# The first norm's scale and shift as columns, applied where the transposed tiles leave PSUM

## The chip, the cores and the metric

One core of a Trainium2 chip runs the whole kernel. The metric is the device time of one execution in microseconds (us). TensorE (PE) multiplies, VectorE (DVE), ScalarE (ACT) and GpSimd (POOL) do the work on rows of numbers, and SyncE (SP) issues the transfers (DMA).

## The reference

A transformer block in float32: a layer norm whose scale and shift come from a condition `c`, attention over the last 512 cached keys, a second norm of the same kind, and a gated feed-forward layer. Only the first norm matters here:

```
mod = (silu(c) @ w_mod).reshape(1, 6, 1, 576)       # c: 1 x 576, w_mod: 576 x 3456
sa, ca, ga, sb, cb, gb = mod[:, 0], ..., mod[:, 5]
h = layernorm(x) * (1 + ca) + sa                    # x: 2048 x 576
x = x + ga * attention(h)                           # 32 heads of 128, q = h @ wq
```

## The kernel before

**Blocks and layout.** The 2048 rows of `x` are four blocks of 512 (b = 0 to 3), each of four tiles of 128 rows (t = 0 to 3). The 576 channels are four chunks of 128 and a tail of 64 (k = 0 to 4); the tail is kept twice, on both halves of the 128 partitions. The projection to q needs the normed block with channels on partitions, `hTs[b]`, split in two parts whose sum is the float32 value: `hi` (rounded to the fast matmul format, fp32r) and `lo` (the rest). `pairs_a` multiplies them with a split of `wq`, chunk by chunk in the order lo, hi with k ascending, so `qproj` can begin as soon as chunk 0 is there.

**The steps.** Attention is a loop over steps n, four steps to a pair of a head and a block (a unit); there are 128 units and N = 512 steps. In step n PE does a quarter of the q projection of the unit after next (`qproj`), the scores of step n + 2 (`scores`), the transposes of the probabilities of step n (`transp`) and a quarter of the product with the values of the unit before (`pv`). DVE takes the row maximum (`neg`), the rest of the split (`ptt`, and `qt` after each fourth quarter of `qproj`), ACT the exponentials (`pp`) and the rounded parts. `at_n` and `at_late` put other work at the head or at the end of a step. `ps_qp` is one PSUM bank, so the next unit's projection waits until DVE has read the one before. `st` has four banks, `ot` two, `wo` one.

**Order.** Until step 8 each engine runs its instructions in the order of the program text (`Ordered`). From then on the scheduler may move instructions, except that those given to `keep_order` or `pin` stay behind the instruction written in front of them on their engine.

**The first norm, blocks 0 and 1.** `silu(c)` is made as five columns `cexp` and spread by ACT to 128 equal columns, `sbc`. `mod_mm` multiplies `sbc` (stationary) with rows of `w_mod` (`WM`, moving, 288 columns at a time), once for the scale (m = 1) and once for the shift (m = 0), 10 products each; a float32 product counts as two instructions. The result is the row of 576 numbers on all partitions. `ln_scaled` norms a tile on ACT and multiplies it by the scale row on DVE or POOL. `ln_channels` transposes chunk by chunk. The shift row is turned into five columns `scol` by small transposes, and `ln_shifted` adds the column while the chunk leaves PSUM: ACT writes `hi`, DVE writes `lo` out of PSUM. Block 1 is done in steps 2 to 6 (`ln_scaled` at the end of steps 2 and 3, `chunks1` in steps 5 and 6).

**Blocks 2 and 3.** `norm_block` puts the statistics, `ln_apply` (DVE subtracts and multiplies, POOL multiplies by the scale row and adds the shift row), `ln_ends` (ACT copies the tail) and `ln_transpose` (a tile at a time; four chunks in one PSUM bank, the tail in `wo`) into the 34 steps ahead of n1 = N / 2 = 256. The second half of the units, which reads these blocks, has its projections from step n1 - 7 on.

**Background.** From step 9 on jobs split later weights (`bg_sums` and `bg_split` on POOL and ACT), with the tiles `xs[b]` of finished blocks as room.

Of the kernel before, what the change touches and what calls it, by code (L numbers as in the profile page):

```python
# [44 lines left out]
def adaln_block_kernel(ctx: ExitStack, tc: tile.TileContext, x, k_cache, v_cache, wq, wo, w_gate, w_up, w_down,  # L45
                       c, w_mod, out):
    early = [True]
    nc = Ordered(tc, early, tc.nc)
# [20 lines left out]
    const = ctx.enter_context(tc.tile_pool(name="const", bufs=1))  # L69
# [30 lines left out]
    def f32(ap):  # L100
        return ap.bitcast(F32)
# [66 lines left out]
    xs = []  # L168
# [5 lines left out]
        t = slice(0, TPB) if t is None else t  # L174
        keep_order(nc.sync.dma_start(xs[b][:, t], xf[b][:, t]))

    LN, HH = {}, {}

    def ln_stats(b, t, hold=False):
        if t == 0 and b % 2 == 0:  # L180
# [38 lines left out]
    def ln_apply(b, t, scale_, shift_, mul, add):  # L219
        mv, y = LN[b][:2]  # L220
        h = h_tile("h")
        nc.vector.tensor_scalar(h, xs[b][:, t, :], mv[:, t, 0:1], y[:, t : t + 1], op0=OP.subtract, op1=OP.mult)
        mul.tensor_mul(h, h, scale_)
        add.tensor_add(h, h, shift_)
        HH[b, t] = h

    ENDS = {}

    def ln_ends(b, t):
        ENDS[b, t] = wp.tile([P, 2, TAIL], F32, tag="hd", name="hd", bufs=2)  # L230
        keep_order(nc.scalar.activation(ENDS[b, t], HH[b, t][:, None, NC * P :].to_broadcast([P, 2, TAIL]), AF.Copy))

    def ln_transpose(b, t):
        main, tail = hTs[b]
        h, ends = HH.pop((b, t)), ENDS.pop((b, t))
        cols = slice(t * P, (t + 1) * P)
        p, pt = ps_pt(), ps_wo()
        for k in range(NC):
            nc.tensor.transpose(p[:, k * P : (k + 1) * P], h[:, k * P : (k + 1) * P], ident)
        nc.tensor.transpose(pt[:, :P], ends.rearrange("p s d -> p (s d)"), ident)  # L240
        src = p.rearrange("p (k q) -> p k q", k=NC)
        keep_order(nc.scalar.activation(main[:, :NC, cols], src, AF.Copy))
        nc.vector.tensor_sub(main[:, NC:, cols], src, f32(main[:, :NC, cols]))
        keep_order(nc.scalar.activation(tail[:, 0, cols], pt[:, :P], AF.Copy))
        nc.vector.tensor_sub(tail[:, 1, cols], pt[:, :P], f32(tail[:, 0, cols]))
# [63 lines left out]

    sbc = at.tile([P, NC + 1, P], F32, tag="qt", name="sbc", bufs=2)
    extra = at.tile([P, 4 * P], F32, tag="rb", name="extra", bufs=2)
    scale, shift = mod_rows("scale"), mod_rows("shift")
    WM, EARLY, HN, NMR = {}, {}, {}, {}

    def load_mod(m, ks):
# [3 lines left out]
            kk = P if k < NC else TAIL  # L321
            nc.sync.dma_start(WM[m][:kk, k, :], w_mod[k * P : k * P + kk, m * D : (m + 1) * D])

    def mod_mm(m, ks, p2):
        for k in ks:
            kk = P if k < NC else TAIL
            for j in range(2):
                nc.tensor.matmul(p2[j], sbc[:kk, k, :], WM[m][:kk, k, j * D2 : (j + 1) * D2],
                                 start=(k == 0), stop=(k == NC))

    def ln_scaled(b, t, eng):
        h = h_tile("h")
        nc.scalar.activation(h, xs[b][:, t, :], AF.Identity, scale=LN[b][1][:, t : t + 1],
                             bias=NMR[b][:, t : t + 1])
        eng.tensor_mul(h, h, scale)
        HN[b, t] = h

    def ln_tail(b, t):
        e = extra[:, t * P : (t + 1) * P].rearrange("p (s d) -> p s d", s=2)
        nc.gpsimd.tensor_copy(e, HN[b, t][:, None, NC * P :].to_broadcast([P, 2, TAIL]))  # L340

    def ln_channels(b, t, k, p):
        src = HN[b, t][:, k * P : (k + 1) * P] if k < NC else extra[:, t * P : (t + 1) * P]
# [32 lines left out]
    for j in range(2):  # L376
        nc.scalar.activation(scale[:, j * D2 : (j + 1) * D2], p2[j], AF.Copy, bias=1.0)
# [7 lines left out]
    p2 = [ps_wo(), ps_qp()[:, :D2]]  # L385
# [6 lines left out]
    nc.scalar.activation(shift[:, :D2], p2[0], AF.Copy)  # L392
    nc.vector.tensor_copy(shift[:, D2:], p2[1])
    ends = wp.tile([P, 2, TAIL], F32, tag="hd", name="hd", bufs=2)
    nc.scalar.activation(ends, p2[1][:, None, D2 - TAIL :].to_broadcast([P, 2, TAIL]), AF.Copy)
    pc = ps_qp()
    for k in range(NC + 1):
        src = shift[0:1, k * P : (k + 1) * P] if k < NC else ends.rearrange("p s d -> p (s d)")[0:1, :]
        nc.tensor.transpose(pc[:, k : k + 1], src, ident[0:1, 0:1])
    scol = csb  # L400
    nc.vector.tensor_copy(scol, pc[:, : NC + 1])
# [208 lines left out]
    def at_n(n, fn, *args):  # L610
        at_step.setdefault(n, []).append((fn, args))
# [3 lines left out]
    def at_late(n, fn, *args):  # L615
        at_end.setdefault(n, []).append((fn, args))
# [39 lines left out]
    for i in range(3):  # L656
        at_late(i, ln_some, 1, False, (0, 6, 9)[i], (6, 9, 13)[i])
    for t in range(TPB):
        at_late(2 + t // 2, ln_scaled, 1, t, nc.vector if t % 2 else nc.gpsimd)
    for t in range(TPB):  # L660
        at_n(4, ln_tail, 1, t)
    at_n(5, chunks1, (0, 1))
# [20 lines left out]
        for t in range(TPB):  # L683
            at_n(N // 2 - 59 + 8 * b + t, load_x, b, t)

    def norm_block(b, n_stats, n_apply, n_t, step, sc_, sh_, mul, add):
        for t in range(TPB):
            at_n(n_stats + t, ln_stats, b, t)
            at_n(n_apply + t * step, ln_apply, b, t, sc_, sh_, mul, add)
            at_n(n_t + t * step - 1, ln_ends, b, t)  # L690
            at_n(n_t + t * step, ln_transpose, b, t)
        if b % 2:
            for k in range(6):
                at_n(n_stats + TPB + k, ln_some, b, True, 2 * k, 2 * k + 2, True)
        at_n(n_t - 1, new_hT, b)

    n1 = N // 2
# [81 lines left out]
    def bg_view(b, off, shape):  # L779
        n = 1  # L780
        for d in shape:
            n *= d
        v = xs[b].rearrange("p t d -> p (t d)")[:, off : off + n]
        if len(shape) == 1:
            return v
        names = "abc"[: len(shape)]
        return v.rearrange(f"p ({' '.join(names)}) -> p {' '.join(names)}",
                           **{names[i]: shape[i] for i in range(len(shape) - 1)})
# [738 lines left out]
```

## Time and profile before

| | us |
|---|---|
| time, median of 3 runs (3051.73 to 3054.39) | 3053.7 |
| the profiled execution, its time | 3053.7 |
| its span, from the first to the last instruction | 3051.9 |
| PE busy | 3014.0 |
| DVE busy | 2110.7 |
| ACT busy | 1691.8 |
| POOL busy | 1654.8 |

Times inside the execution count from the start of the span. The granted clock is the share of full speed that TensorE was given: 1.00 is 2.4 GHz, 0.50 is 1.2 GHz, values between are means over a stretch that holds both. PEld is TensorE's loading of the stationary operand, which overlaps the products. "Idle before" is the idle time of an engine just ahead of an instruction, with what ended it.

### The profile page before, as it was taken

To read this page: it belongs to the slowest core of one execution; us is meant where nothing else is said; L and a number is where in the kernel's file an instruction comes from. 1 tells how busy PE (TensorE), PEld (TensorE's weight loads), DVE (VectorE), ACT (ScalarE), POOL (GpSimd) and SP (SyncE) were. 2 spreads that over 40 slices of the span, in tenths; PEclk is the share of its full clock that TensorE was granted. 3 is DMA by queue.
4 is the path that set the end of the run, shared out by engine and by line. 5 is a ranking of instruction groups with operands and counts; after the bars stand their busy time and mean duration, and the time that the engine had idled before them with its cause. 6 is when DMAs were issued, how large, how long until landed. Compare 5 with 4: busy or idle time off the path is not lost.

```text
span 3051.9 us, 49183 instructions
## 1 busy us (share of the span) xinstructions
PE 3014.0 (99%) x16639; PEld 2591.7 (85%) x16639; DVE 2110.7 (69%) x3716; ACT 1691.8 (55%) x3430; POOL 1654.8 (54%) x1544
## 2 busy tenths in 40 slices
PE   8999999999999999999999999999999999999998
PEld 6888888887888788888999988888888888888887
DVE  5666666677666666667888867666666866666667
ACT  5666667656666666555444654444444545444442
POOL 2343457735577787411555127666655666555654
PEclk9999999999999999999999999999999999999999
DMA  3677777776687777775447656555655565555453
GB/s 111 187 197 199 207 228 216 242 207 180 190 244 228 238 243 250 215 216 180 182 161 306 236 177 187 160 150 159 185 145 143 164 189 140 146 145 143 138 156 98
DMA packets 485788, 571.32 MB, mean 187 GB/s; under 512 B 52000, under 2 KB 434208, under 8 KB 476832
## 3 DMA queue, kind: packets, MB, share of 16 engines
q1 hardware_dynamic: 484400, 567.65, 61.8%
q8 instruction: 132, 2.16, 0.3%
q14 instruction: 120, 0.98, 0.1%
q10 hardware_dynamic: 1136, 0.53, 0.1%
HBM read 394.33 MB, written 173.70 MB: 186 GB/s over the span
## 4 chain that ended last, share of the span: by engine, by line
PE 91%; DVE 3%; POOL 2%; issue 1%; DMA 1%; ACT 1%; SPq 0%; POOLq 0%; DVEq 0%; ACTq 0%
PE a L36 21%; PE st L36 18%; PE qp L36 13%; PE w L36 12%; PE ot L36 11%; PE c L36 10%; PE b L36 5%; DVE x L36 1%; POOL x L36 1%; PE wo L36 0%; DVE v L36 0%; POOL hl L36 0%; POOL vs L36 0%; DVE neg L36 0%; DMA rb<-rscr 0%
## 5 line engine op out<-in xcount | busy, mean ns | idle before, releaser
L36 DVE TENSOR_TENSOR x<-w,x 128x288 f32<-128x288 f32 x980 | 424.0, 451 | 239.2 <-PE w L36 238.2
L36 PE MATMUL a<-hc,sw 128*128 128x512 f32 x2016 | 584.5, 395 | 4.3 <-DVE v L36 4.3
L36 DVE TENSOR_REDUCE neg<-st 128x1 f32<-128x512 f32 x512 | 352.3, 688 | 276.2 <-PE st L36 275.4
L36 ACT ACTIVATE ptt<-st 128x512 fp32r<-128x512 f32 x512 | 306.1, 598 | 398.8 <-PE st L36 398.0
L36 PE MATMUL ot<-ptt,vs 128*128 128x512 f32 x1536 | 486.7, 425 | 1.8 <-DVE ptt L36 1.8
L36 PE MATMUL qp<-hTm,wa 128*128 128x512 f32 x1536 | 444.9, 398 | 8.3 <-DVE qt L36 6.0
L36 PE MATMUL st<-kt,qt 128*128 128x512 f32 x1536 | 443.7, 395 | 0.4 <-ACT pp L36 0.4
L36 DVE TENSOR_TENSOR ptt<-st,ptt 128x512 fp32r<-128x512 f32 x512 | 351.9, 687 | 129.5 <-ACT ptt L36 129.0
L36 PEld LDWEIGHTS a<-hc,sw 128*128 128x128 f32 x2016 | 354.6, 188 | 45.7 <-DVE v L36 5.7
L36 ACT ACTIVATE pp<-st,neg 128x512 f32<-128x512 f32 x512 | 350.7, 685 | 49.6 <-DVE neg L36 48.6
L36 ACT ACTIVATE sw<-sr 128x384 fp32r<-128x384 f32 x504 | 257.3, 518 | 188.2 <-issue 92.1
L36 PEld LDWEIGHTS qp<-hTm,wa 128*128 128x128 f32 x1536 | 286.1, 189 | 78.6 <-DVE qt L36 12.4
L36 PEld LDWEIGHTS w<-wh,hl 128*128 128x128 f32 x1776 | 297.7, 188 | 59.1 <-DVE x L36 9.4
L36 POOL TENSOR_TENSOR sw<-sr,sw 128x256 fp32r<-128x256 f32 x252 | 189.3, 752 | 289.8 <-ACT sw L36 289.0
L36 PEld LDWEIGHTS st<-kt,qt 128*128 128x128 f32 x1536 | 287.2, 188 | 65.2 <-ACT pp L36 1.1
L36 PE MATMUL w<-wh,hl 128*128 128x288 f32 x1776 | 328.9, 295 | 5.4 <-DVE x L36 5.2
L36 PEld LDWEIGHTS st<-ident,pp 128*128 128x128 f32 x2048 | 254.9, 140 | 73.8 <-DVE ptt L36 2.9
L36 POOL TENSOR_TENSOR x<-x 128x256 f32<-128x256 f32 (+3 forms) x334 | 246.8, 759 | 119.7 <-DMA x<-in_B_w_up_dram 65.2
L36 PE MATMUL st<-ident,pp 128*128 128x128 f32 x2048 | 308.1, 273 | 2.8 <-DVE ptt L36 2.8
L36 PE MATMUL c<-hc,sw 128*128 128x512 f32 x1008 | 304.5, 395 | 0.0
L36 PEld LDWEIGHTS ot<-ptt,vs 128*128 128x128 f32 x1536 | 253.4, 191 | 30.3 <-DVE ptt L36 3.6
L36 DVE TENSOR_TENSOR sw<-sr,sw 128x256 fp32r<-128x256 f32 x252 | 179.1, 711 | 143.9 <-ACT sw L36 143.8
(224 smaller groups left out, 5068.3 us busy)
## 6 DMA issues: line engine op xcount, KB each, us to landing
sr<-wsc SPq DMA_DIRECT2D x504, 192.0 KB
wh<-dsc SPq DMA_DIRECT2D x144, 288.0 KB
dsc<-x SPq DMA_DIRECT2D x34, 1008.0 KB
vr<-oscr SPq DMA_DIRECT2D x32, 1024.0 KB
rb<-rscr SPq DMA_DIRECT2D x126, 256.0 KB
wsc<-x SPq DMA_DIRECT2D x36, 896.0 KB
oscr<-ov SPq DMA_DIRECT2D x63, 512.0 KB
wosc<-x SPq DMA_DIRECT2D x32, 1008.0 KB
```

The source lines that it names most:

```text
L36: i = got(*args, **kw)
```

## The change

The scale and the shift are made as columns from the start, and both are applied to the transposed chunks.

- `mod_cols` takes the place of `mod_mm`: the rows of `w_mod` are now stationary, 128 columns at a time, and one column of `cexp` moves. For each k that is four products with 128 stationary columns and two with the 64 of the tail, written to the upper and the lower half of the partitions; 30 products for the scale and 30 for the shift, all into one bank of `wo`. `sbc`, the rows, the small transposes and `ends` are gone. `gcol` (1 + scale) and `scol` are read out of that bank by DVE.
- `ln_norm` norms a tile on DVE or ACT and does nothing else. In block 0 and 1 the tiles alternate between the two, in blocks 2 and 3 all are ACT's. `ln_tail` (POOL copies the tail) now serves all blocks.
- `ln_shifted` writes a chunk as a float32 tile `u` = p * gcol + scol (ACT, out of PSUM), then `hi` (a rounded copy: by ACT out of PSUM, or by DVE or POOL from `u`), then `lo` = u - hi on DVE, both inputs in SBUF. `u` lies in the room of the block's own `x`.
- Blocks 2 and 3 go chunk by chunk as well: norms and tails at steps n1 - 19 to n1 - 16 and n1 - 9 to n1 - 6, one chunk a step at n1 - 15 to n1 - 11 and n1 - 5 to n1 - 1, `hi` by POOL. `ln_apply`, `ln_ends`, `ln_transpose` and `norm_block` are gone. Each chunk uses the single bank `wo`.

```diff
-    def mod_mm(m, ks, p2):
+    def mod_cols(m, ks, p):
         for k in ks:
             kk = P if k < NC else TAIL
-            for j in range(2):
-                nc.tensor.matmul(p2[j], sbc[:kk, k, :], WM[m][:kk, k, j * D2 : (j + 1) * D2],
-                                 start=(k == 0), stop=(k == NC))
+            for c in range(NC):
+                nc.tensor.matmul(p[:, c : c + 1], WM[m][:kk, k, c * P : (c + 1) * P], cexp[:kk, k : k + 1],
+                                 start=(k == 0), stop=(k == NC), skip_group_check=True)
+            for i in range(2):
+                nc.tensor.matmul(p[i * TAIL : (i + 1) * TAIL, NC : NC + 1], WM[m][:kk, k, NC * P :],
+                                 cexp[:kk, k : k + 1], start=(k == 0), stop=(k == NC), skip_group_check=True)
...
-    def ln_scaled(b, t, eng):
-        h = h_tile("h")
-        nc.scalar.activation(h, xs[b][:, t, :], AF.Identity, scale=LN[b][1][:, t : t + 1],
-                             bias=NMR[b][:, t : t + 1])
-        eng.tensor_mul(h, h, scale)
-        HN[b, t] = h
+    def ln_norm(b, t, eng):
+        h = HN[b, t] = h_tile("h")
+        mv, y = LN[b][:2]
+        if eng == "vector":
+            pin(nc.vector.tensor_scalar(h, xs[b][:, t, :], mv[:, t, 0:1], y[:, t : t + 1], op0=OP.subtract, op1=OP.mult))
+        else:
+            pin(nc.scalar.activation(h, xs[b][:, t, :], AF.Identity, scale=y[:, t : t + 1], bias=NMR[b][:, t : t + 1]))
...
-    def ln_shifted(b, k, p):
+    def ln_shifted(b, k, p, eng):
         main, tail = hTs[b]
         hi, lo = (main[:, k, :], main[:, NC + k, :]) if k < NC else (tail[:, 0, :], tail[:, 1, :])
-        nc.scalar.activation(hi, p, AF.Identity, bias=scol[:, k : k + 1])
-        nc.vector.scalar_tensor_tensor(lo, p, scol[:, k : k + 1], f32(hi), op0=OP.add, op1=OP.subtract)
+        u = bg_view(b, k % 4 * BLK if b < 2 else (1 + k % 3) * BLK, [BLK])
+        keep_order(nc.scalar.activation(u, p, AF.Identity, scale=gcol[:, k : k + 1], bias=scol[:, k : k + 1]))
+        if eng == "scalar":
+            keep_order(nc.scalar.activation(hi, p, AF.Identity, scale=gcol[:, k : k + 1], bias=scol[:, k : k + 1]))
+        else:
+            pin(getattr(nc, eng).tensor_copy(hi, u))
+        pin(nc.vector.tensor_sub(lo, u, f32(hi)))
...
-    nc.scalar.activation(sbc, cexp[:, :, None].to_broadcast([P, NC + 1, P]), AF.Copy)
-    p2 = [ps_wo(), ps_qp()[:, :D2]]
-    mod_mm(1, range(NC + 1), p2)
+    mp = ps_wide()
+    mod_cols(1, range(NC + 1), mp[:, : NC + 1])
...
-        ln_scaled(0, t, nc.vector)
+        ln_norm(0, t, "vector" if t % 2 else "scalar")
         ln_tail(0, t)
+    nc.vector.tensor_scalar(gcol, mp[:, : NC + 1], 1.0, None, op0=OP.add)
...
-    mod_mm(0, range(3), p2)
+    mod_cols(0, range(NC), mp[:, NC + 1 :])
     for t in range(TPB):
         for k in range(NC + 1):
             ln_channels(0, t, k, cols[k])
-        if t == 0:
-            mod_mm(0, (3, 4), p2)
...
+        if t == 1:
+            mod_cols(0, (NC,), mp[:, NC + 1 :])
+    nc.vector.tensor_copy(scol, mp[:, NC + 1 : 2 * NC + 2])
     new_hT(0)
     for k in range(NC + 1):
-        ln_shifted(0, k, cols[k])
+        ln_shifted(0, k, cols[k], "scalar" if k % 2 else "vector")
...
-        at_late(2 + t // 2, ln_scaled, 1, t, nc.vector if t % 2 else nc.gpsimd)
+        at_late(2 + t // 2, ln_norm, 1, t, "vector" if t % 2 else "scalar")
...
-    norm_block(2, n1 - 34, n1 - 18, n1 - 14, 2, scale, shift, nc.gpsimd, nc.gpsimd)
-    norm_block(3, n1 - 30, n1 - 9, n1 - 6, 2, scale, shift, nc.gpsimd, nc.gpsimd)
+    def chunk(b, k):
+        p = ps_wide()
         for t in range(TPB):
+            ln_channels(b, t, k, p)
+        ln_shifted(b, k, p, "gpsimd")
+
+    for b, n in ((2, n1 - 19), (3, n1 - 9)):
+        at_n(n + 4, new_hT, b)
+        for t in range(TPB):
+            at_n(n + t, ln_norm, b, t, "scalar")
+            at_n(n + t, ln_tail, b, t)
+        for k in range(NC + 1):
+            at_n(n + 4 + k, chunk, b, k)
```

## Rows read from the trace of the kernel before

**Rows 1.** Busy time by stage: stretch, its length, engines, PEclk, DMA share, GB/s
```profile
0.00:45.00 45.00, 37.76 (x174) 29.92 (x174) 26.32 (x79) 19.57 (x37) 9.94 (x18) 0.92 0.54 157
45.00:64.00 19.00, 12.80 (x58) 9.66 (x57) 11.96 (x18) 12.23 (x23) 5.59 (x7) 0.82 0.18 47
...
660.00:700.00 40.00, 37.72 (x184) 30.36 (x183) 32.91 (x69) 21.16 (x49) 21.95 (x22) 0.96 0.70 204
700.00:760.00 60.00, 59.90 (x326) 49.32 (x325) 46.17 (x79) 40.06 (x96) 31.15 (x35) 1.00 0.67 180
```
**Rows 2.** Chain of waits of the opening: start, us, what it is on
```profile
8.69 1.30 PE wo L36 x2
...
22.03 0.33 PE st L36 x3
...
23.75 0.70 ACT hTm L36
...
24.48 0.76 DVE hTm L36
...
25.37 5.05 PE qp L36 x14
```
**Rows 3.** Timeline of PE around the change to 64 rows: start, length, instruction
```profile
13.16 0.65 PE L36 MATMUL wo<-wm,sbc 128*128 128x288 f32 x2
13.64 0.65 PE L36 MATMUL qp<-wm,sbc 128*128 128x288 f32 x2
14.22 0.75 PE L36 MATMUL wo<-wm,sbc 64*128 64x288 f32 x2
14.81 0.64 PE L36 MATMUL qp<-wm,sbc 64*128 64x288 f32 x2
```
**Rows 4.** Timeline of the weight loads: pairs of loads, nothing queued ahead of them
```profile
8.65 0.50 PEld L36 LDWEIGHTS wo<-wm,sbc 128*128 128x128 f32 x2 [2.54 <-issue]
...
20.10 0.29 PEld L36 LDWEIGHTS wo<-wm,sbc 64*128 64x128 f32 x2 [0.39 <-issue]
```
**Rows 5.** Instructions of tile wm: duration min/median/max in ns, first and last start
```profile
L36 PEld LDWEIGHTS wo<-wm,sbc x20: 183/190/337, 8.7 to 20.2; 128*128 128x128 f32 x16, 64*128 64x128 f32 x4
```
**Rows 6.** Busy time by stretch, as in rows 1, for the granted clock
```profile
8.60:11.00 2.40, 2.31 (x5) 1.77 (x6) 2.13 (x11) 0.00 (x0) 0.00 (x0) 0.50 1.06 296
...
12.00:14.00 2.00, 2.00 (x10) 1.47 (x8) 0.16 (x2) 0.00 (x0) 0.00 (x0) 1.00 1.08 380
...
26.00:27.00 1.00, 1.00 (x4) 0.81 (x3) 1.00 (x2) 1.00 (x3) 0.00 (x0) 0.50 0.07 16
```
**Rows 7.** Chain of waits of steps 2 to 6, where block 1 is normed
```profile
45.04 1.64 ACT h L36 x2
...
46.70 1.31 DVE h L36
...
54.26 0.78 ACT pp L36 x2
...
60.03 1.09 PE ot L36 x4
```
**Rows 8.** Chain of waits ahead of the middle, where block 2 is normed
```profile
687.50 1.40 DVE h L36
688.89 0.61 DVE qt L36
...
689.55 0.97 PE qp L36 x3
```
**Rows 9.** Instructions of tile h, as in rows 5
```profile
L36 ACT ACTIVATE h<-x,ln_a,ln_y x8: 855/857/868, 15.8 to 50.1; 128x576 f32<-128x576 f32 x8
...
L36 DVE TENSOR_SCALAR h<-x,mv,ln_y x8: 570/662/1479, 683.5 to 723.0; 128x576 f32<-128x576 f32 x8
```
**Rows 10.** Groups of instructions with shapes: count, busy us, mean ns, idle before
```profile
L36 DVE TENSOR_TENSOR vh<-vr,vh 128x512 fp32r<-128x512 f32 x128 | 119.2, 932 | 12.4 <-ACT vh L36 11.7
...
L36 POOL COPY te<-ts 128x256 f32<-128x256 f32 x14 | 5.2, 400 | 10.9 <-PE w L36 9.1 <-DMA ts<-scr 1.8
```

More of the change, by code (lines that the diff above doesn't have):

```diff
@@ L175, in load_x, with bg_view @@
         keep_order(nc.sync.dma_start(xs[b][:, t], xf[b][:, t]))
-    LN, HH = {}, {}
+    def bg_view(b, off, shape):
+        n = 1
+        for d in shape:
+            n *= d
+        v = xs[b].rearrange("p t d -> p (t d)")[:, off : off + n]
+        if len(shape) == 1:
+            return v
+        names = "abc"[: len(shape)]
+        return v.rearrange(f"p ({' '.join(names)}) -> p {' '.join(names)}",
+                           **{names[i]: shape[i] for i in range(len(shape) - 1)})
+    LN = {}
     def ln_stats(b, t, hold=False):
@@ L217, in ln_some @@
                 pin(i)
-    def ln_apply(b, t, scale_, shift_, mul, add):
-        mv, y = LN[b][:2]
-        h = h_tile("h")
[L222 to L245, printed above, removed]
     def load_a(w, n0):
@@ L308, in new_hT @@
         hTs[b] = (main, tail)
-    sbc = at.tile([P, NC + 1, P], F32, tag="qt", name="sbc", bufs=2)
     extra = at.tile([P, 4 * P], F32, tag="rb", name="extra", bufs=2)
-    scale, shift = mod_rows("scale"), mod_rows("shift")
+    gcol, scol = const.tile([P, NC + 1], F32, name="gcol"), csb
     WM, EARLY, HN, NMR = {}, {}, {}, {}
@@ L338, in ln_tail, with extra_of @@
+    def ln_norm(b, t, eng):
[5 more added lines that the diff above has]
+            pin(nc.scalar.activation(h, xs[b][:, t, :], AF.Identity, scale=y[:, t : t + 1], bias=NMR[b][:, t : t + 1]))
+    def extra_of(b):
+        return extra if b < 2 else bg_view(b, 0, [4 * P])
     def ln_tail(b, t):
-        e = extra[:, t * P : (t + 1) * P].rearrange("p (s d) -> p s d", s=2)
+        e = extra_of(b)[:, t * P : (t + 1) * P].rearrange("p (s d) -> p s d", s=2)
@@ L340, in ln_tail @@
         nc.gpsimd.tensor_copy(e, HN[b, t][:, None, NC * P :].to_broadcast([P, 2, TAIL]))
     def ln_channels(b, t, k, p):
-        src = HN[b, t][:, k * P : (k + 1) * P] if k < NC else extra[:, t * P : (t + 1) * P]
+        src = HN[b, t][:, k * P : (k + 1) * P] if k < NC else extra_of(b)[:, t * P : (t + 1) * P]
         nc.tensor.transpose(p[:, t * P : (t + 1) * P], src, ident)
-    def ln_shifted(b, k, p):
+    def ln_shifted(b, k, p, eng):
         main, tail = hTs[b]
         hi, lo = (main[:, k, :], main[:, NC + k, :]) if k < NC else (tail[:, 0, :], tail[:, 1, :])
-        nc.scalar.activation(hi, p, AF.Identity, bias=scol[:, k : k + 1])
-        nc.vector.scalar_tensor_tensor(lo, p, scol[:, k : k + 1], f32(hi), op0=OP.add, op1=OP.subtract)
+        u = bg_view(b, k % 4 * BLK if b < 2 else (1 + k % 3) * BLK, [BLK])
[5 more added lines that the diff above has]
+        pin(nc.vector.tensor_sub(lo, u, f32(hi)))
@@ L370, in adaln_block_kernel @@
     nc.vector.tensor_mul(cexp, cexp, csb)
-    nc.scalar.activation(sbc, cexp[:, :, None].to_broadcast([P, NC + 1, P]), AF.Copy)
-    p2 = [ps_wo(), ps_qp()[:, :D2]]
-    mod_mm(1, range(NC + 1), p2)
+    mp = ps_wide()
+    mod_cols(1, range(NC + 1), mp[:, : NC + 1])
     for t in range(1, TPB):
         ln_stats(0, t)
-    for j in range(2):
-        nc.scalar.activation(scale[:, j * D2 : (j + 1) * D2], p2[j], AF.Copy, bias=1.0)
     ln_some(0, False, 0, 13)
     for t in range(TPB):
-        ln_scaled(0, t, nc.vector)
+        ln_norm(0, t, "vector" if t % 2 else "scalar")
         ln_tail(0, t)
+    nc.vector.tensor_scalar(gcol, mp[:, : NC + 1], 1.0, None, op0=OP.add)
     EARLY["sq"] = split_a_hi(EARLY["q", 0])
@@ L384, in adaln_block_kernel @@
     cols = [ps_pt(), ps_pt(), ps_pt(), ps_ot(), ps_ot()]
-    p2 = [ps_wo(), ps_qp()[:, :D2]]
-    mod_mm(0, range(3), p2)
+    mod_cols(0, range(NC), mp[:, NC + 1 :])
     for t in range(TPB):
@@ L389, in adaln_block_kernel @@
             ln_channels(0, t, k, cols[k])
-        if t == 0:
-            mod_mm(0, (3, 4), p2)
[L392 to L401, printed above, removed]
+        if t == 1:
+            mod_cols(0, (NC,), mp[:, NC + 1 :])
+    nc.vector.tensor_copy(scol, mp[:, NC + 1 : 2 * NC + 2])
     new_hT(0)
     for k in range(NC + 1):
-        ln_shifted(0, k, cols[k])
+        ln_shifted(0, k, cols[k], "scalar" if k % 2 else "vector")
     ln_stats(1, 0)
@@ L412, in chunks1 @@
                 ln_channels(1, t, k, p)
-            ln_shifted(1, k, p)
+            ln_shifted(1, k, p, "gpsimd" if k % 2 else "scalar")
     RA, SA, KR, KS, VR, VS = {}, {}, {}, {}, {}, {}
@@ L684, in adaln_block_kernel @@
             at_n(N // 2 - 59 + 8 * b + t, load_x, b, t)
-    def norm_block(b, n_stats, n_apply, n_t, step, sc_, sh_, mul, add):
-        for t in range(TPB):
[L688 to L697, printed above, removed]
-    norm_block(2, n1 - 34, n1 - 18, n1 - 14, 2, scale, shift, nc.gpsimd, nc.gpsimd)
-    norm_block(3, n1 - 30, n1 - 9, n1 - 6, 2, scale, shift, nc.gpsimd, nc.gpsimd)
+    n1 = N // 2
+    for t in range(TPB):
+        at_n(n1 - 34 + t, ln_stats, 2, t)
+        at_n(n1 - 30 + t, ln_stats, 3, t)
+    for k in range(7):
+        at_n(n1 - 26 + k, ln_some, 3, True, 2 * k, 2 * k + 2, True)
+    def chunk(b, k):
+        p = ps_wide()
+        for t in range(TPB):
+            ln_channels(b, t, k, p)
+        ln_shifted(b, k, p, "gpsimd")
+    for b, n in ((2, n1 - 19), (3, n1 - 9)):
+        at_n(n + 4, new_hT, b)
+        for t in range(TPB):
+            at_n(n + t, ln_norm, b, t, "scalar")
+            at_n(n + t, ln_tail, b, t)
+        for k in range(NC + 1):
+            at_n(n + 4 + k, chunk, b, k)
     TQ = D2 - 2 * P
@@ L777, in adaln_block_kernel @@
     BG = {}
[L779 to L788, printed above, removed]
     def bg_load(k, rooms):
```

1 line of the change is left out of this document (removed).

## The prediction

> **What bounds the kernel.** I read the stages first. PE is busy almost all the time, so a change is worth only what it does to PE's idle stretches and to its clock. Where the first norm touches the kernel there are three places [rows 1]: the opening (0 to 45 us: 7.2 us idle, clock 0.92), block 1's norm (45 to 64: 6.2 us idle, clock 0.82) and the 40 us ahead of the middle (2.3 us idle, clock 0.96). From 700 to 760, where the other tiles of blocks 2 and 3 are done, PE idles 0.1 us; DVE, ACT and POOL work taken away there buys nothing. Then I read the chain of waits in each place. In the opening it is PE itself: the products with `w_mod` from 8.69, transposes, then ACT and DVE making the first chunk at 23.75 and 24.48, and the first projection at 25.37 [rows 2]. Around block 1 it runs over ACT, DVE and back to PE, and 60.03 is where PE becomes steady [rows 7]. Ahead of the middle, DVE's norm of a tile (1.40) stands in front of the `qt` split, and PE waits for that until 689.55 [rows 8].
>
> **The opening.** Ten k (five for the scale, five for the shift) now cost what their weight loads cost, since one column moves per load. The trace shows the load: a pair takes 0.29 us at full clock and 0.50 at half [rows 4], one alone 0.19 and 0.34 [rows 5], so loads follow each other at 0.10 to 0.11 at full clock and at 0.165 or more at half; I take 0.21 for the latter, twice the full rate, because the single load also grows with the clock. A tail load has half the columns; I take half. A float32 product is two loads, so a k is 8 loads of 128 columns and 4 of 64: 8 x 0.105 + 4 x 0.053 = 1.05 us at full clock, 8 x 0.21 + 4 x 0.105 = 2.1 at half. Before, a k was two pairs 0.48 apart, 0.97 at full clock [rows 3].
>
> Second, the change of shape. Where 128 rows give way to 64, pairs start 0.58 and 0.59 apart instead of 0.48 [rows 3]: 0.2 us for one change, because the next load isn't drawn ahead. The new k goes from 128 columns to 64 and back, two changes, 20 in all. A change of columns isn't in the trace; bounds are 0 and 0.4 (at half clock), I take 0.2, the nearest row: 4.0 us. The Trainium skill, TensorEngine Tiling (Array Packing), Key Properties, states that changing the tiling mode drains TensorE, of columns as of rows. By that the lower bound of 0 falls; the row of the change of rows agrees with 0.2 us.
>
> Third, the clock, which decides. PE comes out of an idle stretch at 0.50 and reaches 1.00 while the 288-column products stream; it is back at 0.50 at 26, after the transposes, the five one-column transposes and 1.9 us of waiting [rows 6]. How it answers to a stream of loads with one column each, the trace doesn't show. I take it that it doesn't rise, because what PE did whenever it rose was to stream products of 128 to 512 columns close on each other, and here the array takes in one column per 0.1 to 0.2 us.
>
> At half clock: 8.69 + 10 x 2.1 + 4.0 = 33.7. Ten of the transposes stand ahead of the last k (0.11 each at full clock [rows 2], 0.22 at half): 35.9. Draining the last product and DVE's copy to `scol`, 0.4 as before the 23.75: 36.3. Then chunk 0: ACT's `u` 0.70, DVE's copy to `hi` 0.5 (estimate; between nothing and the 0.57 that the 576-wide one-input DVE form takes alone [rows 9]), `lo` 0.7, hand-overs 0.1. The projection begins at 38.3, where it was 25.37: **12.9 us later** (with 0.165 a load and no cost of change 4.4; with 0.4 a change 17). The norms themselves are ready earlier, as neither `sbc` nor a scale row is waited for, but the transposes stand behind the products on PE, so that is worth nothing. Later chunks are hidden: ACT needs 0.7 to 1.4 us a chunk, PE at half clock 1.3.
>
> **Block 1.** The norm of tile 0 on ACT (0.86 [rows 9]) and of tile 1 on DVE (0.6) replace two of ACT in a row (1.64) and a multiply of 1.31 on DVE with `neg` behind it [rows 7]. Following ACT and DVE in program order from 45.04: `pp` of step 3 can start at 46.5 and that of step 4 (54.26 before) at about 51, 3.3 us earlier. `hi` of chunks 0, 2 and 4 is a second ACT pass of 0.7 that holds the bank, which gives back 1.4 before the last chunk's transposes, at 58.0 for 60.03: **2.0 us less**. Bounds: 4 less (the low clock in this stretch goes too) and 2 more (ACT's three passes on the path, nothing gained ahead).
>
> **The middle.** DVE's eight norms, 0.57 alone and up to 1.48 beside POOL [rows 9], and POOL's sixteen passes over a tile go. ACT takes eight norms of 0.86 and ten `u` of 0.7 for its former parts, at 21.16 of 40 us busy [rows 1]; a norm that stands in front of `pp` or `ptt` on ACT delays a transpose that is due two steps later, so it is covered. The wait that ended at 689.55 goes: 1.8 us. The low clock that follows costs (1 - 0.96) x 40 = 1.6 [rows 1]. **3.4 us less.** Next late is nothing that I find; the statistics leave 0.5 us of idle. POOL's copy to `hi` has 512 numbers, 0.6 to 0.8 by the 256-wide copy's 0.40 [rows 10]. PE's work (20 transposes a block) is the same, no DMA is moved, and no queue passed; the statistics chain has one instruction more (0.2, hidden).
>
> The profiled execution stands at its span + 1.8, and is the median. Sum: 3053.7 + 12.9 - 2.0 - 3.4 = **3061.2**.
>
> **Rivals.** *The clock rises* (the one that isn't slower). One-column products count as work, and PE is at 1.00 from 12 on as before [rows 6]. Then 3.3 us at half clock do 1.3 k (2.5 each with the changes), the other 8.7 take 1.45 each, 12.6: 24.6, + 1.1 + 0.4 + 2.0 = 28.1, 2.7 later than now; without a cost of change 24.4, 1.0 earlier. The time: 3053.7 + 2.7 - 5.4 = 3051.0, down to 3047.3. For it speaks that PE's queue is never empty in that stretch; against it, that the array is.
>
> *DVE waits for POOL.* `lo` is written to stay behind its forerunner on DVE, needs POOL's copy, and POOL runs background jobs of 0.7 to 3 us. Behind `lo` on DVE can stand `neg`, `ptt` and `qt`, and behind `qt` PE's next projection, with some 2 us of cover. Two of the ten chunks (steps 244 and 252) fall into a step with `qt`. If one is late by a POOL job, a wait like the one removed is back, with its low clock: 3.4 us, and the middle gains nothing: 3064.6 with the slow opening, 3054.4 with the other. Against it: POOL loses more work there than it gets, and instructions that aren't pinned may be moved ahead. What the row shows beside POOL is 0.57 against 1.48 for one form [rows 9] and a mean of 0.93 for a split with both inputs in SBUF [rows 10]; `lo` changes from PSUM to that kind. The Trainium skill, SBUF — State Buffer, Who interferes with whom, has a rule that speaks against this: a DVE operation with two SBUF inputs and a POOL one that reads SBUF exclude each other, and the later waits whole. By it each `lo` could cost up to one POOL instruction more; the 1.48 agrees.
>
> **Chances and range.** Forecast 0.50, the clock rises 0.35, DVE waits 0.15. A measurement of this kernel tells about 0.2%, 6.1 us, from no change. The forecast's own range, from the bounds of the change of shape and of block 1, is 3055 to 3067; two thirds of it lie above 3059.8. Slower: 0.33 + 0.10 = 0.43. Faster by over 6.1 needs the risen clock and every bound at its best: 0.06. The rest, 0.51, is within. The range over all: 3047.3 to 3067.
>
> **What would show it.** Right: clock 0.50 from 8.7 to past 38, loads 0.21 apart, first projection near 38, PE without a gap around 690 and at 1.00 there. Wrong: clock 1.00 from 12 on (the second case), gaps of PE in the middle ended by DVE with POOL's copy ahead of it (the third), or 60.03 not earlier against the first projection.

## The result, and the profile after

| | before | after |
|---|---|---|
| time, median of 13 runs each, us | 3054.0 (3051.7 to 3056.7) | 3061.3 (3057.7 to 3064.1) |
| the profiled execution, its time | 3053.7 | 3061.6 |
| its span | 3051.9 | 3059.8 |

The ratio is 1.0022, with a 95% interval of 1.0013 to 1.0031: slower, but by a fifth of a percent. The medians lie 7.3 us apart, the two profiled executions 7.9.

Busy time by stretch in the kernel after (stretch, its length, then busy us and instructions of PE, PEld, DVE, ACT and POOL, granted clock, DMA share, GB/s):

```profile
0.00:45.00 45.00, 39.28 (x199) 36.29 (x200) 16.12 (x52) 10.57 (x16) 5.67 (x15) 0.66 0.50 157
...
670.00:710.00 40.00, 39.38 (x202) 31.70 (x202) 32.38 (x68) 26.43 (x57) 11.08 (x17) 1.00 0.75 208
710.00:770.00 60.00, 59.23 (x321) 48.70 (x320) 45.71 (x68) 41.33 (x86) 28.99 (x41) 1.00 0.72 188
8.60:12.00 3.40, 3.40 (x20) 3.37 (x19) 2.92 (x16) 0.00 (x0) 0.00 (x0) 0.50 1.05 342
12.00:16.00 4.00, 4.00 (x25) 3.94 (x25) 1.14 (x3) 1.63 (x2) 1.06 (x4) 0.50 1.15 310
...
33.00:36.00 3.00, 1.66 (x8) 1.28 (x7) 1.43 (x3) 2.46 (x4) 0.00 (x0) 0.50 0.00 0
36.00:40.00 4.00, 4.00 (x12) 3.18 (x12) 3.75 (x8) 2.97 (x5) 0.90 (x1) 0.62 0.01 2
```

The opening's mean clock is 0.66 where it was 0.92 [rows 1]; it is at half speed from 8.6 to 39 us, and PE is busy without a gap in 8.6 to 16. Before came into its products at half speed too, and rose at about 12 [rows 6]. The 40 us ahead of the middle (they lie 10 us later now) have lost their low clock and most of PE's idle time: 0.6 us where it was 2.3. The next 60 have gained idle time: 0.8 where it was 0.1.

The chain of waits of the opening, after (start, us, what it is on):

```profile
8.28 10.56 PE wo L36 x60
...
19.09 8.47 PE wo L36 x48
27.55 0.83 PE st L36 x3
...
29.88 2.10 PE wo L36 x12
31.98 0.83 PE st L36 x3
...
35.67 5.03 PE qp L36 x14
```

It is PE from end to end: five k of the scale, four of the shift, ten transposes, the fifth k of the shift, ten more transposes. The projection begins at 35.67, not at 25.37 [rows 2], 10.3 us later.

Where the rest went is read from the starts of DVE's row maxima, one for each of the 512 steps. Each number is the difference to the first trace of before (there 34.46, 70.17, 666.39, 770.15 and 1428.09 us for the steps named), the last one that of the spans. A gain in a stage is the difference of two neighbours in a line.

| | step 0 | step 10 | step 230 | step 266 | step 511 | end |
|---|---|---|---|---|---|---|
| after | +10.26 | +8.85 | +9.39 | +6.89 | +5.95 | +7.93 |
| e1, 128 columns move | +1.82 | +1.03 | +0.69 | -1.87 | -4.23 | -2.52 |
| e2, products as rows | -0.31 | -1.46 | -1.68 | -4.15 | -4.54 | -3.92 |
| e3, middle's norms by DVE | +8.64 | +6.16 | +5.71 | +5.16 | +0.72 | +2.77 |
| e4, middle's `hi` by ACT | +10.27 | +8.90 | +8.49 | +5.34 | +0.87 | +2.81 |
| e5, before again | -1.88 | -1.91 | -1.81 | -1.67 | -2.05 | -1.75 |
| e6, rooms kept | +10.27 | +8.85 | +8.67 | +6.03 | +2.11 | +6.42 |
| e7, block 1's `hi` by POOL | +10.00 | +6.85 | +6.75 | +4.30 | +1.93 | +3.76 |
| e8, e2 and e4 | -0.53 | -1.69 | -1.92 | -5.06 | -8.58 | -6.76 |
| e9, e2 and more PE | +4.43 | +1.81 | +1.39 | -1.14 | -2.47 | -2.33 |
| e10, e8 and e7 | -0.36 | -3.52 | -4.21 | -7.49 | -11.69 | -11.15 |
| e11, one tail | +8.51 | +6.11 | +5.89 | +3.41 | +1.63 | +3.37 |

So after, in us: opening +10.3, block 1 -1.4, middle (steps 230 to 266) -2.5. The other 1.6 lie where nothing was changed: +0.5 between steps 10 and 230, -0.9 up to step 511, +2.0 in the feed-forward part. The middle's gain repeats: the six other traces that have after's code there (e1, e2, e6, e7, e9, e11) show 2.45 to 2.64.

The first two columns need care. The first traces of before and after come into the products with `w_mod` at half clock; e1, e2, e3, e5 and e8 to e11 come into them at 1.00. For before alone that is worth 1.9 us (e5). Like against like, the opening of after costs the same: 10.3 at step 0 where both start at half clock, and 10.5 (e3) and 10.4 (e11) against e5 where both start at 1.00.

### The profile page after: what moved, and what is told of

Read it like the earlier page. It is cut to its first block, busy times and chain, and to the rows that moved or that the text cites. A ratio compares the mean times of both kernels' runs of the same rounds, so it can differ in the third digit from the quotient of the medians.

```text
span 3059.8 us, 49316 instructions
## 1 busy us (share of the span) xinstructions
PE 3025.8 (99%) x16714; PEld 2608.8 (85%) x16714; DVE 2091.3 (68%) x3704; ACT 1698.6 (56%) x3420; POOL 1655.1 (54%) x1546
## 3 DMA queue, kind: packets, MB, share of 16 engines
q1 hardware_dynamic: 484400, 567.65, 62.9%
## 4 chain that ended last, share of the span: by engine, by line
PE 90%; DVE 3%; DMA 2%; POOL 2%; issue 1%; ACT 1%; SPq 0%; POOLq 0%; DVEq 0%; ACTq 0%
PE a L36 21%; PE st L36 17%; PE qp L36 13%; PE w L36 13%; PE ot L36 11%; PE c L36 10%; PE b L36 5%; DVE x L36 1%; PE wo L36 1%; POOL x L36 1%; DMA rscr<-rs 0%; DMA rb<-rscr 0%; SPq L36 0%; DVE neg L36 0%; ACT pp L36 0%
## 5 line engine op out<-in xcount | busy, mean ns | idle before, releaser
L36 POOL TENSOR_TENSOR sw<-sr,sw 128x256 fp32r<-128x256 f32 x252 | 206.0, 818 | 296.0 <-ACT sw L36 267.8
L36 PEld LDWEIGHTS qp<-hTm,wa 128*128 128x128 f32 x1536 | 285.8, 189 | 76.9 <-DVE qt L36 12.9
```

The lines of the kernel that those rows point to most:

```text
L36: i = got(*args, **kw)
```

## The experiments

They ran on three other chips, where the median of before was 3050.9 us (e1 to e4), 3049.7 (e5 to e8) and 3050.0 (e9 to e11). A time is compared with the one of its own chip; a kernel that ran once is read by its trace alone.

**e1: the same products, but 128 equal columns move.** Theory: one-column products don't bring the clock up. Rival: it is the number of loads and the changes of shape.

```diff
-                nc.tensor.matmul(p[:, c : c + 1], WM[m][:kk, k, c * P : (c + 1) * P], cexp[:kk, k : k + 1],
+                nc.tensor.matmul(p[:, c * P : (c + 1) * P], WM[m][:kk, k, c * P : (c + 1) * P], sbc[:kk, k, :],
...
-                nc.tensor.matmul(p[i * TAIL : (i + 1) * TAIL, NC : NC + 1], WM[m][:kk, k, NC * P :],
-                                 cexp[:kk, k : k + 1], start=(k == 0), stop=(k == NC), skip_group_check=True)
+                nc.tensor.matmul(q[i * TAIL : (i + 1) * TAIL], WM[m][:kk, k, NC * P :],
+                                 sbc[:kk, k, :], start=(k == 0), stop=(k == NC), skip_group_check=True)
```

> The changed kernel with 128 equal columns of cexp moving in each of the 60 products instead of one; the weight loads, their number and their order stay, the columns are read out of the first column of each group. Theory (the clock): the granted clock rises by about 12 to 13 us as in the kernel before; 3.3 us at half clock do 1.3 k at 2.56 us (12 times 0.213), the other 8.7 take about 1.3 each; the first projection begins near 26.5 instead of 35.66 and the time falls by about 9 us, to 3052 (ratio to before about 0.999). Rival (it is the loads, or the change between 128 and 64 columns, that take the time, whatever the clock is): nothing is gained, since no load goes away and each product streams more; the first projection stays near 36 or comes later, 3061 to 3065.

Measured: 3051.5 us, ratio 1.0001 (0.9991 to 1.0010). The chain and two stretches:

```profile
8.24 1.13 PE wo L36 x8
9.37 0.37 PE qp L36 x4
9.74 1.09 PE wo L36 x8
...
27.10 5.16 PE qp L36 x14
...
11.00:12.00 1.00, 1.00 (x11) 0.88 (x8) 0.83 (x6) 0.00 (x0) 0.00 (x0) 1.00 1.03 336
12.00:16.00 4.00, 4.00 (x35) 3.12 (x34) 1.41 (x5) 1.63 (x2) 1.06 (x4) 1.00 1.14 292
```

A k with the same 12 loads and the same changes of shape takes 1.46 us instead of 2.11, although each product moves 128 times as many columns: the clock is at 1.00 throughout. The projection starts at 27.10 (26.5 was expected). This trace came into the products at 1.00, which after didn't, so by itself it could be the state it started from. e3 and e11 answer that.

**e3: the middle's norms on DVE again**, and, by chance, an opening that started at full clock.

```diff
-            at_n(n + t, ln_norm, b, t, "scalar")
+            at_n(n + t, ln_norm, b, t, "vector")
```

> The changed kernel with the norms of blocks 2 and 3 on DVE instead of ACT. Theory (the stall ahead of the middle came from POOL's passes over the same tiles, beside which DVE's norm took up to 1.48 us): each norm now takes about 0.57 to 0.75, no wait of PE for qt above 1 us near 700, time within 2 us of the changed kernel. Rival (any norm on DVE in front of qt stalls PE): a gap of 1.5 us or more and a stretch at clock 0.50 near 700 come back, 3 us more.

Measured: 3056.5 us in one run. Busy time by stretch in e3:

```profile
8.10:11.00 2.90, 2.84 (x29) 2.82 (x29) 2.56 (x13) 0.00 (x0) 0.00 (x0) 1.00 1.06 319
11.00:12.00 1.00, 1.00 (x10) 0.98 (x9) 0.83 (x6) 0.00 (x0) 0.00 (x0) 0.61 1.03 373
12.00:16.00 4.00, 4.00 (x24) 3.95 (x24) 1.12 (x3) 1.62 (x2) 1.06 (x4) 0.50 1.14 299
...
710.00:770.00 60.00, 58.58 (x308) 46.69 (x308) 45.13 (x70) 36.53 (x78) 27.28 (x39) 1.00 0.67 183
```

The loads of one k, in e3 while its clock was at 1.00 and in after at 0.50 (start, length, instruction), and a wait of PE in e3's middle:

```profile
9.32 1.18 PEld L36 LDWEIGHTS wo<-cexp,wm 128*128 128x128 f32 x12
```
```profile
10.35 2.08 PEld L36 LDWEIGHTS wo<-cexp,wm 128*128 128x128 f32 x12
```
```profile
PE wo L36 <- ACT x L36: 0.5, 1, 0.5
```

The opening, the same code as in after, begins at 1.00 and falls to 0.50 at about 11.2, while PE is 100% busy with one-column products. It is not a late answer to the wait ahead of the products either: e1 begins as late (8.24, here 8.16) after the same kind of wait, and stays at 1.00. At 1.00 a k took 1.2 us, at 0.50 2.1; over ten k the clock is worth about 9 of the opening's 10.3 us (an estimate from these two rows).

In the middle the gain is 0.55 instead of 2.50, well outside what the other traces show. The stall of 1.8 us does not come back as one wait, nor does the low clock. PE idles 1.4 us in 710 to 770 where after idles 0.8; what is new is a wait of 0.5 for ACT's pass out of the single bank `wo`. The rest of what is lost shows in no row of idle time: read from the starts of PE's products it is in short waits, none above 0.25 us. So most of the middle's gain hangs on ACT norming these tiles; how DVE's norms bring the short waits about is not shown.

**e11: the second 64-column product of a k left out** (in all k but the first; the upper half's scale and shift are then partial sums).

```diff
-            for i in range(2):
+            for i in range(2 if k == 0 else 1):
                 nc.tensor.matmul(p[i * TAIL : (i + 1) * TAIL, NC : NC + 1], WM[m][:kk, k, NC * P :],
-                                 cexp[:kk, k : k + 1], start=(k == 0), stop=(k == NC), skip_group_check=True)
+                                 cexp[:kk, k : k + 1], start=(k == 0), stop=(k == NC or i == 1), skip_group_check=True)
```

> The changed kernel, but the second product of 64 stationary columns (for the upper half of the partitions) is made for the first k only; the other eight are left out, so the upper half's scale and shift are partial sums. The sum of the forecast took the two products one behind the other, 0.42 us a k at half clock, and 0.4 us for two changes of shape on top; the changed kernel takes 2.11 us a k in all, 0.4 less. Theory: the two products run side by side and the changes cost their 0.2 us each; then leaving one out saves nothing, at most 0.05 us a k, and the products take 10.5 and 8.4 us as in the changed kernel. Rival: they run one behind the other and a change costs nothing; then it saves 0.21 us a k, 1.7 us in all, and the first ends at about 18.0 us and the projection starts 1.7 us earlier.

Measured: 3057.1 us in one run. Weight loads (start, length, instruction, idle before) of the shift's first four k, in after and in e11, with e11's clock, and the four loads of 64 columns of one k in after:

```profile
19.08 8.39 PEld L36 LDWEIGHTS wo<-cexp,wm 128*128 128x128 f32 x48 [0.35 <-DVE gcol L36]
```
```profile
16.33 8.37 PEld L36 LDWEIGHTS wo<-cexp,wm 128*128 128x128 f32 x42 [0.34 <-DVE gcol L36]
...
8.10:11.00 2.90, 2.90 (x28) 2.84 (x28) 2.56 (x13) 0.00 (x0) 0.00 (x0) 1.00 1.06 327
11.00:12.00 1.00, 1.00 (x8) 0.97 (x8) 0.83 (x7) 0.00 (x0) 0.00 (x0) 0.60 1.01 376
12.00:16.00 4.00, 4.00 (x20) 3.94 (x20) 1.02 (x3) 1.63 (x2) 1.06 (x4) 0.50 1.15 302
```
```profile
10.04 0.29 PEld L36 LDWEIGHTS wo<-cexp,wm 128*64 128x64 f32 x4
```

Four k at half clock take 8.37 us of loads with 42 instructions where after takes 8.39 with 48: the second product of 64 columns is free. The two run side by side: their four loads, 0.18 to 0.23 us each, take 0.29 together. The first five k were shorter than after's (8.03 us for 10.56) only because they, too, began at 1.00: e3, with all 60 instructions, took 8.14. At about 11.2 the clock fell to 0.50, with PE 100% busy: the second time that this fall is seen.

**e2: the old products as rows, the rest of the change kept.**

```diff
-    mod_cols(1, range(NC + 1), mp[:, : NC + 1])
+    p2 = [ps_wo(), ps_qp()[:, :D2]]
+    mod_mm(1, range(NC + 1), p2)
...
+    row_cols(scale, ends1, pc[:, : NC + 1])
+    row_cols(shift, ends0, pc[:, NC + 1 : 2 * NC + 2])
+    nc.vector.tensor_copy(gcol, pc[:, : NC + 1])
+    nc.vector.tensor_copy(scol, pc[:, NC + 1 : 2 * NC + 2])
```

> The rest of the change without its products: scale and shift are made as rows as in the kernel before (20 products of 288 columns), both rows are turned into columns by ten small transposes, and everything behind that is the changed kernel. Theory: the first projection begins at 25.5 to 26.5, what block 1 and the middle gain stays (1.4 and 2.5 us in the traces), so the time is 3050 to 3052, below the kernel before by 2 to 4 us. Rival (the later parts cost time by themselves, the gain in the middle being only noise of the trace): 3054 or more.

Measured: 3047.9 us, ratio 0.9989 (0.9979 to 0.9998).

The first projection in the chain of e2, and in e5 (before again) by the timeline of PE:

```profile
24.98 5.15 PE qp L36 x14
```
```profile
23.52 2.05 PE L36 MATMUL qp<-hTm,wa 128*128 128x512 f32 x4 [1.85 <-DVE hTm L36]
```

The projection starts at 24.98 (25.5 to 26.5 was expected), 0.4 earlier than in the first trace of before. But that trace came in at half clock. Against e5, which starts at 1.00 as e2 does, it is 1.5 later: the way over rows and small transposes, with the passes behind it, costs that much. Block 1 (-1.2) and the middle (-2.5) gain as in after. So the loss of 10 us lies in the one-column products, and applying the columns late gains.

**e4: `hi` of blocks 2 and 3 by ACT out of PSUM instead of by POOL.**

```diff
-        ln_shifted(b, k, p, "gpsimd")
+        ln_shifted(b, k, p, "scalar")
```

> The changed kernel with hi of blocks 2 and 3 by a second pass of ACT out of PSUM instead of POOL's copy from u. If DVE's wait for POOL's copy costs PE anything, the 0.8 us that PE idles from 710 to 770 fall to 0.1 as in the kernel before; if not, they stay or grow, because ACT holds the bank 0.7 us longer.

Measured: 3056.6 us in one run. First the waits of DVE and of PE from 710 to 770 in after (who waited for whom: us in all, times, longest), two of the subtractions, and what stands behind the second; then that stretch in e4:

```profile
DVE hTm L36 <- POOL hTm L36: 2.1, 4, 0.7
...
PE qp L36 <- DVE qt L36: 0.8, 1, 0.8
...
717.64 1.21 DVE L36 TENSOR_TENSOR hTm<-x,hTm 128x512 fp32r<-128x512 f32 x1 [0.71 <-POOL hTm L36]
720.37 0.71 DVE L36 TENSOR_TENSOR hTm<-x,hTm 128x512 fp32r<-128x512 f32 x1
720.97 0.71 DVE L36 SCALAR_TENSOR_TENSOR qt<-qp,qt 128x512 fp32r<-128x512 f32 x1
721.74 0.96 PE L36 MATMUL qp<-hTm,wa 128*128 128x512 f32 x3 [0.77 <-DVE qt L36]
```
```profile
710.00:770.00 60.00, 59.82 (x324) 49.13 (x323) 42.65 (x69) 46.54 (x94) 20.79 (x30) 1.00 0.69 191
```

In after DVE waits for POOL's copy of a chunk four times. PE waits once, for the split of q (`qt`) that stands behind these subtractions on DVE: 0.8 us, all that PE idles in this stretch. With ACT's copy PE idles 0.2, and the middle gains 3.15 (3.1 and 3.3 in e8 and e10, which have that copy too).

**e7: `hi` of block 1 by POOL alone.**

```diff
-            ln_shifted(1, k, p, "gpsimd" if k % 2 else "scalar")
+            ln_shifted(1, k, p, "gpsimd")
```

> The changed kernel, with the rounded copy of every chunk of block 1 by GpSimd instead of GpSimd and ScalarE by turns. It tests the term of the sum that says that ScalarE's second pass over a chunk (0.78 us, three of them) gives back part of block 1's gain, because it holds the bank that the next chunk's transposes wait for. Theory: the last chunk's transposes, 2.6 us earlier against the opening in the changed kernel, come another 0.7 to 1.4 us earlier, and the row maximum of step 10 follows by as much, or by less where the half clock lasts over the same stretch. Rival: DVE's subtraction waits for GpSimd's copy, which takes 0.6 to 0.9 us beside its background work, so the row maxima behind it come no earlier or later by up to 1 us.

Measured: 3057.5 us in one run. The last chunk's transposes in the chain of after and of e7, each with two stretches behind it:

```profile
67.69 1.09 PE ot L36 x4
...
67.00:70.00 3.00, 2.31 (x8) 1.95 (x9) 1.39 (x2) 2.38 (x4) 0.62 (x1) 0.50 0.03 1
70.00:73.00 3.00, 3.00 (x11) 2.52 (x10) 1.91 (x3) 2.22 (x5) 1.29 (x1) 0.50 0.90 196
```
```profile
66.64 0.95 PE ot L36 x4
...
67.00:70.00 3.00, 3.00 (x12) 2.51 (x11) 1.78 (x3) 1.69 (x4) 2.79 (x4) 0.50 0.10 33
70.00:73.00 3.00, 3.00 (x15) 2.44 (x14) 2.58 (x3) 1.14 (x3) 0.83 (x1) 0.97 0.82 228
```

The transposes start 1.05 us earlier (0.8 against the opening). The row maximum of step 10 comes 1.7 us earlier against the opening, more than that, because the half clock is over at 70.2 and not at 73.2. e3, e9 and e11 have after's code in block 1 and gain 2.4 to 2.6 there, where after and the others with that code gain 0.8 to 1.4. The low clock lasts 3.4 us in all in these three (in e3 0.69 in 64.5 to 68, 0.84 in 68 to 72) and 6.8 in after and the others. So, from single traces that agree among themselves, ACT's second passes cost about 0.7 (e7 and e10 gain 3.2), and the length of the half clock 1.1. What decides its length is open.

**e5 and e6: how far single traces agree, and the rooms of the two rows.**

> The kernel before, profiled a second time, to see what of a difference between two single traces is chance. Theory: the stretch from the last row maximum of the attention to the end (1623.8 us in the first trace of before, 1625.5 to 1625.9 in three of the four traces with columns) repeats within 0.3 us, and so is a property of the kernel; the stall of 2.4 us with half clock behind it near 1040 us does not repeat, or moves, and is chance. Rival: the last stretch itself varies by 2 us from run to run; then the 2.0 us by which the changed kernel lost there are nothing that the change did.

> The changed kernel, but the two rows of 576 numbers that it no longer needs (scale, shift) are reserved again and filled with zeros by GpSimd at the start; nothing reads them. Everything else keeps its place in the order, only the places of the other tiles in SBUF move back to those of before. Theory of the place: the last stretch, the feed-forward part, goes from 1625.5 to 1625.9 us back to 1623.8 to 1624.4, as in the two kernels that hold these rows. Rival (the last stretch goes by chance or by another part of the change): it stays at 1625.5 to 1625.9. The opening stays as in the changed kernel, 8.6 to 10.3 us longer than before, unless the clock comes out of its first stretch at full speed and stays there.

```diff
+    for tag in ("scale", "shift"):
+        tc.nc.gpsimd.memset(mod_rows(tag), 0.0)
```

e5, 3052.0 us in one run. The opening is 1.9 us shorter than in the first trace of before, with a stretch at half clock less in it; behind it the lines agree within 0.4, and the feed-forward part takes 1624.1 where it was 1623.8. The wait behind a transfer near step 370, 2.4 us in the first trace with half clock after it, is there again, against the expectation, and the part around it is 0.4 shorter.

e6, 3060.1 us in one run: step 10 is that of after to 0.01, and after's 0.96 us between steps 58 and 64 are gone, as they are in every other trace, so these are chance. The feed-forward part takes 1628.1 instead of 1625.8, 1.6 of it at a wait near 2480, with a low clock behind it that no other trace has there, and the rest in small steps; without that wait it is no shorter than in after. The rooms aren't the reason for the 2.0.

**e9: e2 with 70 more products on PE.**

```diff
-    row_cols(scale, ends1, pc[:, : NC + 1])
-    row_cols(shift, ends0, pc[:, NC + 1 : 2 * NC + 2])
+    for _ in range(8):
+        row_cols(scale, ends1, pc[:, : NC + 1])
+        row_cols(shift, ends0, pc[:, NC + 1 : 2 * NC + 2])
```

> The version with the old products as rows (e2), in which the ten small transposes that turn the rows into columns are done eight times over, so that TensorE runs 70 products and 70 loads more before the first projection: as many as the changed kernel has. Open is why the stretch behind the last row maximum takes 1625.5 to 1625.9 us in every trace with one-column or 128-column products (60 of them, in after, e1, e3, e4, e7), and 1623.8, 1624.1 and 1624.4 in the two of before and in e2; most of the difference grows evenly from 380 to 1600 us behind the last row maximum. Theory: it hangs on where TensorE's instructions lie, and so on their number. Then the stretch grows evenly here too and takes 1625.4 us or more. Rival: it hangs on something else of the changed kernel (the places of tiles); then it takes 1623.8 to 1624.5. The opening is 4 to 8 us longer than in e2 by the transposes added, which is not the question.

Measured: 3051.4 us in one run; the feed-forward part takes 1624.0. That is what the rival expected: the number of PE's instructions isn't the reason either. All kernels with products as columns took 1625.5 to 1625.9 (e6 aside), those with rows 1623.8 to 1624.5, except e8 with 1625.6. Why is open.

This run has something else to show, the clock over its 80 small transposes and behind them:

```profile
21.75:26.75 5.00, 4.99 (x81) 4.91 (x80) 0.00 (x0) 0.00 (x0) 0.00 (x0) 1.00 0.10 34
27.20:30.00 2.80, 0.87 (x2) 0.78 (x3) 1.86 (x4) 2.80 (x5) 0.00 (x0) 0.50 0.00 0
```

**e8 and e10: what gained, without what lost.** e8 is e2 with e4's edit; e10 is e8 with e7's edit.

> The version that keeps what gained and undoes what lost: scale and shift as rows by the old wide products, turned into columns afterwards, the rest as in the changed kernel, but the rounded copies of blocks 2 and 3 by ScalarE out of PSUM instead of GpSimd. Theory: opening as before or up to 1 us shorter, block 1 1.4 to 2 us, the middle 3.1 us shorter (2.5 with GpSimd), in all 3048.5 to 3049.5 beside 3053.7 of before, a ratio of 0.9982 to 0.9990. Rival: the middle's 0.6 us between the two makers of the rounded copy is chance between two single traces; then the ratio is that of the version with GpSimd's copies, 0.9989.

> The version of e8 (old products as rows, norms and shift as columns, rounded copies of blocks 2 and 3 by ScalarE), with the rounded copies of block 1 all by GpSimd as in e7. Theory: e7's 2.0 us at the row maximum of step 10 add to e8's gains, so 3.7 us less than before by step 10 and 7 us less behind the middle, a ratio of 0.9975 to 0.9985. Rival: without the slow opening the half clock of block 1 ends elsewhere and takes the 2 us back; then the ratio is e8's 0.9993 again, within 0.0005.

e8: 3048.3 us beside 3049.7 of before on that chip, ratio 0.9993 (0.9984 to 1.0002). e10: 3045.2 beside 3050.0, ratio 0.9985 (0.9976 to 0.9994). e10's interval lies below 1, and its medians 4.8 us apart; its ratio is the lowest of these kernels, though the interval overlaps those of e2 and e8. The expectation of e8 was missed: its interval reaches over 1 and holds e2's 0.9989 as well, and the 0.6 us of ACT's copy can't be told in the medians, though three traces show them.

e10's trace, of the fastest of its eleven runs, gains 3.5 by step 10 (3.7 expected) and 7.5 by step 266 (7 expected). 1.9 and 1.7 of these are the half clock with which the first trace of before began: against e5 they are 1.6 and 5.8. The 4.2 beyond that, up to step 511, are mostly the wait near step 370 (3.2), which about half of the traces lack, whatever the kernel.

## Why the prediction was right, and where its terms were not

The median came out at 3061.3 where 3061.2 was predicted, on the mechanism of the forecast: a clock that stays down in the opening, against smaller gains in block 1 and in the middle. That the number fits to 0.1 us is luck. Against the profiled execution the cost of the opening was put 2.6 too high, the gains of block 1 and of the middle 0.6 and 0.9 too high, and 1.6 us lie outside the change; the errors cancel. The range had a slip: with 0.4 a change and block 1 2 us longer the sum gives 3069, not 3067, which changes nothing here.

**The opening: 12.9 predicted, 10.3 measured.** The step that decided was the third, the clock, and it held: 0.50 from 8.6 to past 38, loads of 128 columns start 0.213 us apart in the trace. The rival of a rising clock is excluded by that trace, and e1, e3 and e11 show that it is the single column. The mis-sized term is the second, the change of shape: 2.5 us a k were predicted, 2.1 + 0.4; a k takes 2.11 in all (10.56 us for five, 8.47 for four, 2.10 for one). Half of the 0.4 too much is the two products of 64 columns: they run side by side, as e11 shows, where the sum took them one behind the other. The other half is left for the changes themselves, which then cost about 0.1 each and not 0.2. That is 3.9 us less over ten k. Against it stand 1.2 us that the forecast overlooked: it let chunk 0's `u` follow 0.4 us behind the last product, but the last ten transposes stand behind that product (31.98 in the chain), at half clock, and `u` starts at 33.55, as its row in the timeline of after shows:

```profile
33.55 1.45 ACT L36 ACTIVATE x<-st,csb,gcol 128x512 f32<-128x512 f32 x2 [16.25 <-PE st L36]
```

The start was 0.4 earlier, and PE waits 0.3 for DVE to read `gcol` (the shift's products go to the same bank). 38.3 - 3.9 + 1.2 - 0.4 + 0.3 is 35.5; the projection is at 35.67.

The 0.1 is an estimate: a k costs 8 loads of 0.213, 1.70, and 0.41 for the rest; two loads of half the columns, taken at half the time, are 0.21 of that, so about 0.2 are left for the two changes of a k, half of what the sum took. The Trainium skill, TensorEngine Tiling (Array Packing), Key Properties, states that a change of tiling mode drains TensorE; the trace agrees as far as that a change costs something.

**Block 1: 2.0 predicted, 1.4 measured.** The chain ahead went as worked out: against the opening, the last chunk's transposes are 2.6 us earlier (67.69 less 10.3, for 60.03 [rows 7]), where 2.0 was expected. What was not foreseen is behind them. From there on PE is steady, and the half clock still lasts 5.5 us (to 73.2), where in before it lasted 2.9 (60.03 to 62.9); half of that difference, 1.3, is lost, and 1.2 is what is missing. The bound "4 less" stood on the low clock going away, and no bound stood on its lasting longer. In e3, e9 and e11 the half clock is 3.4 us shorter, and the gain is 2.4 to 2.6. The second pass that "gives back 1.4" cost about 0.7 (e7).

**The middle: 3.4 predicted, 2.5 measured.** DVE's norm ahead of the `qt` split [rows 8] went, with it the idle time, and the clock is 1.00 as the sum took it. "Next late is nothing that I find" was wrong: it is the rival in which DVE waits for POOL, in small. DVE waits for POOL's copy, and PE for the `qt` behind it, 0.8 us, not the 3.4 of a stall with low clock. e4 takes it away and gives 3.15 of the 3.4. How little margin there was is seen in e3: the wait and the low clock are gone there as well, and short waits of PE take all but 0.55 back. The copy itself was priced right, 0.62 us for 0.6 to 0.8. What was left out of the sum is how long `lo` takes beside POOL: 0.69 us alone, but 1.19 to 1.76 in five of ten, those that begin while POOL works, as the two rows of 717 and 720 show. The Trainium skill, SBUF — State Buffer, Who interferes with whom, has a DVE instruction with two SBUF inputs and a POOL one that reads SBUF exclude each other for the whole instruction. The trace agrees in size: the surplus of 0.5 to 1.1 us is at most about one POOL instruction there (0.7 to 1.1 us). The 1.48 that the prediction put beside this rule was of a norm with one such input; it is these rows that bear on it.

**Outside.** Nothing was foreseen for places where nothing is changed, and there 1.6 us came about: 0.96 of chance at steps 58 to 64, and 2.0 in the feed-forward part, whose cause e6 and e9 did not find, less 1.4 in small steps elsewhere.

## What to carry to other kernels

Products that move one column are cheap by count only: before replacing wide products with them, look at the clock that such a stream has had in a trace, and price the loads at half speed as well. A factor that belongs to a channel can be applied after the transposition, where it is one operand of a pass that is there anyway; here that gained even with a few small transposes to turn it into a column (e2, e10). A change that gains in two places and loses in one should be cut there, and traces to compare should start at the same clock, or 2 us of chance are read as gain. e10 keeps the gains and is 0.15% faster than before, where the whole was 0.22% slower.

## What the runs showed of the hardware

- One-column float32 products, close behind each other for 20 us, did not hold the clock: it was 0.50 all through after's, and where it began at 1.00 it fell to 0.50 in the midst of them, at 11.2 us (e3, e11). The same loads with 128 columns moving stayed at 1.00 (e1). A k of twelve such loads took 1.2 us at 1.00 (e3) and 2.1 at 0.50 (after). One-column transposes with a single row loaded 0.063 us apart held 1.00 for their 5 us, and it was at 0.50 by 27.2, right behind them (e9); whether these transposes or the 0.45 us without work behind them made it fall is open.
- Two products of 64 columns to the two halves of the partitions run side by side: 8.37 us with one of them, 8.39 with both (e11, after).
- How long the low clock behind a stall lasts isn't fixed by the code: block 1's was 6.8 us in after and 3.4 in e3 with the same instructions there, worth 1.1 us.
